# Loading later batches in four-head pieces, one piece per value sum, with q and k one more batch ahead

## The chip, the cores and the metric

The kernel runs on one core of a Trainium2 chip. The metric is device time in microseconds (us) for one launch, lower is better. Times of whole runs come from runs without a profiler; everything that is said of single instructions comes from one profiled execution.

## The reference

Eight batches of twelve heads, 448 positions and 64 channels per head go through a ReLU-squared attention without softmax; the result, seen as 3584 tokens of 768 channels, goes through a gated feed-forward block (GEGLU).

```python
scores = (1 / sqrt(64)) * q @ k.transpose(0, 1, 3, 2)
attn   = maximum(scores, 0) ** 2 / 448
x      = (attn @ v)                   # -> [3584, 768]
u      = gelu(x @ w_gate) * (x @ w_val)   # [3584, 1536], gelu with erf
out    = u @ w_out                    # [3584, 768]
```

Inputs and outputs are f32; the kernel computes in bf16 with f32 sums.

## The kernel before

**Tiling.** TensorE is used as four 64x64 quarters: two row halves (called PE0 and PE1 in the planner) that work at the same time, each with two column halves. A batch's feed-forward block is twelve chunks `fc` of 128 hidden channels. For each chunk `add_gate_value` (L411) adds a gate sum (g = 0), from which ScalarE makes the GELU `gel` (L429), and a value sum (g = 1), which VectorE multiplies into `uT` (L434). After the twelve chunks come output tiles of 128 tokens (`add_out`, L450), each in two halves that ScalarE copies into `osb` (L472, three buffers) and SyncE sends out as two DMAs (L477). By the loop at L516 batches 0 to 7 are followed by 2, 4, 3, 4, 3, 4, 3 and 5 output tiles.

**Attention.** A batch's attention is done during the feed-forward block of the batch before it: 21 score units (`add_scores`, L310; ReLU `rl` on ScalarE at L336, square on VectorE at L342) and six value products (`add_values`, L367; copy to `xT` on VectorE at L391).

**Loads.** All loads are GpSimd DMAs that cast f32 to bf16, in one queue in program order (`load`, L169; `load_qk`, L189; `load_v`, L204). Batches 0 and 1 come in pieces of two or four heads between the weights. Each later batch comes as four whole DMAs: q, k and two halves of v. q and k share a tile `qk16` of which there are two buffers, `v16` has two buffers as well. Batch b + 2 is put into the queue when the last value product of batch b is put into the work list (L544 to L549), q and k before v.

**Transposes.** Scores need q and k with channels on the partitions (`qkT`, two buffers). Batches 0 to 2 (`EARLY` = 3) are transposed by TensorE (`add_transposes`, L277, copies at L293). From batch 3 on (`add_dma_transposes`, L230) VectorE makes seven copies of `qk16` into `qkr` (L237, one buffer), and one DMA transpose from SyncE (L245) makes `qkT` of it. That transpose needs the buffer of `qkT` that the scores of two batches before have read.

**Order of the work.** The order on each engine is written out ahead of time by a small planner, `run_plan` (L23). Every piece of work is an `Op` with a cost, a list of others that it comes after, a lag and a priority. `PE0` and `POOL` are taken strictly in order; PE1, ACT, DVE and SP take, out of their next 48, the one that can start first, the smaller `prio` first among equals. Loads are given an arrival: bytes at 400 GB/s one after the other, and 2.0 us. A plan's dependence sets only the *order* of the instructions in the program; the semaphore waits on the chip come from the data alone (a tile's writer and readers, a free buffer, and eight semaphores that the loads take in turn, each only when its last load has landed). Each engine then runs its own list strictly in order: an instruction whose data is late holds back all that stand behind it on its engine.

Of the kernel before, what the change touches and what calls it, by code (L numbers as in the profile page):

```python
# [22 lines left out]
def run_plan(queues, pools, arrivals, together):  # L23

    free = {e: 0.0 for e in (*queues, *pools)}
    at = {e: 0 for e in queues}
    dma = last = floor = 0.0

    def ready(op):
        t = 0.0
        if op.after is not None:
            if op.after.start is None:
                return None
            t = op.after.start
        for d in op.deps:
            if d.end is None:
                return None
            t = max(t, d.end + d.lag)  # L40
        return t

    left = sum(map(len, queues.values())) + sum(map(len, pools.values()))
    while left:
        best = None
        for e, ops in queues.items():
            if at[e] < len(ops):
                r = ready(ops[at[e]])
                if r is not None:
                    t = max(r, free[e], floor if e in together else 0.0)  # L50
                    key = (t, 0, free[e])
                    if best is None or key < best[0]:
                        best = (key, e, ops[at[e]])
        for e, ops in pools.items():
            mine = None
            for op in ops[:48]:
                r = ready(op)
                if r is not None:
                    t = max(r, free[e], floor if e in together else 0.0)
                    key = (t, op.prio, free[e])  # L60
                    if mine is None or key < mine[0]:
                        mine = (key, e, op)
            if mine and (best is None or mine[0] < best[0]):
                best = mine
        assert best is not None, "the plan is stuck"
        (t, _, _), e, op = best
        op.start = t
        op.end = t + op.cost
        free[e] = op.end
        if e in together:  # L70
            floor = t
        if op in arrivals:
            dma = max(dma, op.end) + arrivals[op]
            op.lag = dma + 2.0 - op.end
        if e in at:
            at[e] += 1
        else:
            pools[e].remove(op)
        op.emit()
        last = max(last, op.end)  # L80
        left -= 1
    return last
# [3 lines left out]
def kernel(  # L86
# [16 lines left out]
    B, H, S, D = q.shape  # L103
# [3 lines left out]
    NPAIR = H // 2  # L107
# [12 lines left out]
    EARLY = 3  # L120
# [33 lines left out]
    def wait_lower(box):  # L154

        tc.add_manual_dep(nc.tensor.reg_mov(n_reg, 0).ins, box[1].ins.name, SYNC, reason="bank")

    ACT, DVE, POOL, SP = [], [], [], []
    arrivals = {}


# [4 lines left out]
    w12_op, wo_op, head_op = {}, {}, {}  # L166
    qk16, v16 = {}, {}

    def load(nbytes, emit, deps=(), cost=0.7):  # L169
        op = Op("POOL", cost, emit, deps)  # L170
        arrivals[op] = nbytes / 400e3
        POOL.append(op)
        return op
# [15 lines left out]
    def load_qk(b, i, h0, h1, deps=()):  # L189

        src = (q, k)[i]

        def tile_of():
            if b not in qk16:
                qk16[b] = qkv.tile([128, H * S // P * D], bf16, name="qk16", tag="qk16")
            return qk16[b][HALF[i], :]

        op = load(4 * (h1 - h0) * S * D, lambda: nc.gpsimd.dma_start(  # L198
            tile_of().rearrange("p (h x) -> p h x", h=H)[:, h0:h1, :],
            src[b, h0:h1].rearrange("h (p c) d -> p h (c d)", c=SC)), deps)  # L200
        for pr in range(h0 // 2, h1 // 2):
            head_op[b, pr, i] = op

    def load_v(b, h0, h1, deps=()):  # L204

        for i in range(2):
            def emit(i=i):
                if b not in v16:
                    v16[b] = qkv.tile([128, H, VC, D], bf16, name="v16", tag="v16")
                c0 = i * (SC - VC)  # L210
                nc.gpsimd.dma_start(  # L211
                    v16[b][HALF[i], h0:h1, :, :],
                    v[b, h0:h1].rearrange("h (p c) d -> p h c d", c=SC)[:, :, c0:c0 + VC, :])
            op = load(4 * (h1 - h0) * VC * P * D, emit, deps)
            for pr in range(h0 // 2, h1 // 2):
                head_op[b, pr, 2 + i] = op

    def load_heads(b, h0, h1, deps=((), ())):
        load_qk(b, 0, h0, h1, deps[0])
        load_qk(b, 1, h0, h1, deps[0])  # L220
        load_v(b, h0, h1, deps[1])

    qkT, tr_op, r_op = {}, {}, {}

    def qkT_tile(b):
        if b not in qkT:
            qkT[b] = tpool.tile([128, SC * NPAIR, 2 * P], bf16, name="qkT", tag="qkT")
        return qkT[b]

    def add_dma_transposes(b):  # L230

        box = {}

        def emit_copy(c):
            if not box:
                box[0] = lpool.tile([128, SC, H, D], bf16, name="qkr", tag="qkr")
            nc.vector.tensor_copy(  # L237
                box[0][:, c], qk16[b].rearrange("p (h c d) -> p c h d", c=SC, d=D)[:, c])

        copies = [Op("DVE", 0.4, lambda c=c: emit_copy(c),  # L240
                     [head_op[b, 0, 0], head_op[b, 0, 1], tr_op.get(b - 1)], lag=0.1, prio=3)
                  for c in range(SC)]
        DVE.extend(copies)
        r_op[b] = copies
        tr_op[b] = Op("SP", 7.0, lambda: nc.sync.dma_start_transpose(  # L245
            qkT_tile(b)[:, :, :], box[0].rearrange("p c h d -> p (c h d)")),
            [*copies, last_s.get(b - 2)], lag=5.0)
        SP.append(tr_op[b])


# [5 lines left out]
    def ring_dep():  # L256
        return [ring[-FB]] if len(ring) >= FB else []
# [15 lines left out]
    att, xT, last_s = {}, {}, {}  # L273
    t_op, relu_op, sq_op, o_op, x_op = {}, {}, {}, {}, {}
# [136 lines left out]
    def add_gate_value(at, b, fc, g):  # L411

        i, o = divmod(fc * 128, WCH)
        w = (wg, wv)[g][i]
        box = {}

        def emit(r, dc):
            if not box:
                box[0] = psF.tile([128, 512], f32, name="ff", tag="F")
            if r == 1 and dc == 0:  # L420
                wait_lower(box)
            for j in range(2):
                ins = mm(box[0][HALF[j], 0:S], w[HALF[r], dc, o + P * j:o + P * (j + 1)],
                         xT[b][HALF[r], dc, :], r, j, r == 0 and dc == 0, r == 1 and dc == KC - 1)
            box[1] = ins

        def emit_gelu():
            gel[b, fc] = gpool.tile([128, S], bf16, name="gel", tag="gel")
            nc.scalar.activation(gel[b, fc][:, :], box[0][:, 0:S], AF.Gelu)  # L429

        def emit_mult():
            if fc == 0:
                uT[b] = upool.tile([128, FC, S], bf16, name="uT", tag="uT")
            nc.vector.tensor_tensor(uT[b][:, fc, :], gel.pop((b, fc))[:, :],  # L434
                                    box[0][:, 0:S], op=ALU.mult)

        ops = [[Op(f"PE{r}", GS, lambda r=r, dc=dc: emit(r, dc),
                   [w12_op[i][g], x_op[b, dc], *(ring_dep() if r == 0 and dc == 0 else ())], lag=0.24)
                for dc in range(KC)] for r in range(2)]
        if g == 0:  # L440
            done = gel_op[b, fc] = Op("ACT", 0.55, emit_gelu, [ops[1][-1]], lag=0.06, prio=0)
            ACT.append(done)
        else:
            done = u_op[b, fc] = Op("DVE", 0.63, emit_mult, [gel_op[b, fc], ops[1][-1]],
                                    lag=0.1, prio=0)
            DVE.append(done)
        ring.append(done)
        then(at, GS, *ops, done)

# [91 lines left out]

    for at, _, fn, args in work:
        fn(at, *args)
        if fn is add_values and args[1] == NPAIR - 1 and args[0] + 2 < B:  # L544
            b = args[0]
            free = [t_op[b, NPAIR // 2 - 1, i] for i in range(2)] if b < EARLY else r_op[b]
            load_heads(b + 2, 0, H, (free, (o_op[b, NPAIR - 1],)))
            if b + 2 >= EARLY:
                add_dma_transposes(b + 2)  # L549


    def emit_filler():
# [6 lines left out]
    PE0 = [op for _, op in lower]  # L559
# [23 lines left out]
    PE1 = [op for _, op in upper]  # L583

    def emit_warm_up():
        t = psF.tile([128, 512], f32, name="ff", tag="F")
        for _ in range(10):
            for j in range(2):
# [1 line left out]
                                 start=True, stop=True, tile_position=(0, P * j))  # L590
    PE0.insert(0, warm_op)

    run_plan({"PE0": PE0, "POOL": POOL}, {"PE1": PE1, "ACT": ACT, "DVE": DVE, "SP": SP}, arrivals,
             ("PE0", "PE1"))


# [28 lines left out]
```

## Time and profile before

| | |
|---|---|
| time, median of 3 runs | 472.1 us (470.2 to 475.5) |
| time of the profiled execution | 468.75 us, of which the span of its instructions is 467.0 us |
| TensorE busy | 432.0 us, 93% of the span; granted clock 0.979 |
| VectorE, ScalarE busy | 206.2 us (44%), 225.5 us (48%) |
| GpSimd load queue | 36416 packets, 24.38 MB |
| SyncE queue (transposes, outputs) | 31520 packets, 17.90 MB |

How to read the rows that follow. A row of a timeline has start, duration, engine, line, operation, tiles written and read, and in brackets the idle time of the engine before it and what ended it. A row of waits has the engine and line that waited, what it waited for, and then us in total, how often, and the longest. A row of windows has for each engine its busy time and, behind x, its instructions, then the granted clock of TensorE, the share of the DMA engines' time and the GB/s moved. DMA rows have the count, the size in SBUF's type of one, and the median time from issue to landing. PE is TensorE's multiplications, PEld its weight loads, DVE VectorE, ACT ScalarE, POOL GpSimd, SP SyncE (SPq its queue).

### The profile page before, as it was taken

The page shows a single profiled execution, that of the slowest core. Times are in us where ns is not written, and L with a number is a line of the kernel's source. Part 1 is how long each engine was busy: PE and PEld are TensorE (multiplying, and loading weights), DVE is VectorE, ACT ScalarE, POOL GpSimd, SP SyncE. Part 2 cuts the span into 40 slices and gives each one's busy share as a digit, 9 for nine tenths or more (in the row PEclk, how much of TensorE's full clock was granted, in tenths as well). Part 3 has the DMA queues.
Part 4 walks back from the last instruction along what each step waited for, and adds up shares of the span by engine and source line. Part 5 has one row for each costly group of instructions (what it writes and reads, how often), then busy time and mean ns, then how long its engine had stood idle before and what let it go on. Part 6 is the DMA issues. An engine that isn't in the chain of part 4 may idle for free.

```text
span 467.0 us, 19995 instructions
## 1 busy us (share of the span) xinstructions
PE 432.0 (93%) x9360; PEld 370.6 (79%) x9360; DVE 206.2 (44%) x366; ACT 225.5 (48%) x322; POOL 48.9 (10%) x74
## 2 busy tenths in 40 slices
PE   6779999998997999996999959999999999999995
PEld 2547996976896678984999837899999978887895
DVE  1695655554542365443543334534553455312200
ACT  1686554444452555552555525555555555422221
POOL 8546300200002000020000100010000000000000
PEclk9998999999999899998999988999999999999998
DMA  7999999698029900695007950086002300030024
GB/s 101 192 198 198 205 207 193 88 158 136 1 48 167 232 4 3 119 207 85 3 3 132 221 94 1 3 163 129 3 3 54 88 3 4 14 93 3 3 70 102
DMA packets 68019, 43.56 MB, mean 93 GB/s; under 512 B 29024, under 2 KB 64352, under 8 KB 67936
## 3 DMA queue, kind: packets, MB, share of 16 engines
q0 software_dynamic: 36416, 24.38, 36.6%
q1 hardware_dynamic: 31520, 17.90, 18.0%
q8 instruction: 73, 1.20, 1.0%
q14 instruction: 10, 0.08, 0.1%
HBM read 48.76 MB, written 11.01 MB: 128 GB/s over the span
## 4 chain that ended last, share of the span: by engine, by line
PE 70%; DMA 22%; POOL 2%; issue 2%; DVE 2%; ACT 1%; SPq 0%; POOLq 0%; ACTq 0%; DVEq 0%
PE ff L151 64%; DMA qk<-in_k_dram 13%; PE sp L151 5%; DMA qk<-in_q_dram 3%; DMA wv<-in_moe_w_val_dram 2%; DMA out_dram<-osb 2%; DMA v<-in_v_dram 1%; POOL v L211 1%; POOL qk L198 1%; ACT rl L336 1%; DVE attnT L342 1%; DVE uT L434 0%; PE ff L287 0%; DVE qkT L293 0%; DVE qkr L237 0%
## 5 line engine op out<-in xcount | busy, mean ns | idle before, releaser
L151 PE MATMUL ff<-xT,wg 64*64 64x448 bf16 x2304 | 232.5, 356 | 13.9 <-DVE uT L434 9.6
L151 PE MATMUL ff<-xT,wv 64*64 64x448 bf16 x2304 | 232.0, 355 | 2.1 <-issue 2.1
L336 ACT ACTIVATE rl<-sp 128x896 bf16<-128x896 f32 x168 | 152.1, 920 | 126.7 <-PE sp L151 109.2
L151 PEld LDWEIGHTS <-wg 64*64 64x64 bf16 x2304 | 134.5, 109 | 34.1 <-issue 17.6
L151 PE MATMUL ff<-wo,uT 64*64 64x384 bf16 x2688 | 149.8, 323 | 0.3 <-DVE uT L434 0.2
L151 PEld LDWEIGHTS <-wv 64*64 64x64 bf16 x2304 | 134.8, 108 | 16.3 <-issue 1.2
L342 DVE TENSOR_TENSOR attnT<-rl 128x896 bf16<-128x896 bf16 x168 | 103.9, 623 | 89.7 <-ACT rl L336 88.9
L151 PEld LDWEIGHTS <-uT 64*64 64x64 bf16 x2688 | 124.9, 107 | 5.8 <-DVE uT L434 0.6
L151 PE MATMUL sp<-qkT 64*64 64x448 bf16 (+1 forms) x768 | 114.8, 348 | 7.8 <-ACT rl L336 4.7
L434 DVE TENSOR_TENSOR uT<-gel,ff 128x448 bf16<-128x448 bf16 x96 | 59.5, 620 | 78.5 <-PE ff L151 75.7
L151 PE MATMUL ff<-attnT,v 64*64 64x448 bf16 (+1 forms) x768 | 91.1, 338 | 0.0
L429 ACT ACTIVATE gel<-ff 128x448 bf16<-128x448 f32 x96 | 52.1, 543 | 63.5 <-PE ff L151 61.8
L151 PEld LDWEIGHTS <-qkT 64*64 64x64 bf16 x768 | 48.0, 111 | 19.4 <-issue 11.0
L151 PEld LDWEIGHTS <-v 64*64 64x64 bf16 x768 | 48.4, 110 | 4.0 <-issue 0.2
L472 ACT COPY osb<-ff 128x384 f32<-128x384 f32 x56 | 26.7, 477 | 46.3 <-PE ff L151 37.5
L391 DVE TENSOR_SCALAR xT<-ff 128x448 bf16<-128x448 f32 x48 | 29.9, 623 | 36.0 <-PE ff L151 31.3
L211 POOL DMA_DIRECT2D v<-in_v_dram x26 | 17.8, 703 | 245.5 <-PE sp L151 130.5
L287 PEld LDWEIGHTS <-qk 64*64 64x64 bf16 x504 | 14.3, 127 | 8.4 <-DMA qk<-in_k_dram 3.8
L287 PE MATMUL ff<-ident,qk 64*64 64x64 bf16 x504 | 15.2, 213 | 4.9 <-DMA qk<-in_k_dram 2.6
L237 DVE COPY qkr<-qk 128x768 bf16<-128x768 bf16 x35 | 11.5, 354 | 16.0 <-DMA qk<-in_k_dram 9.8
L293 DVE COPY qkT<-ff 128x896 bf16<-128x896 bf16 x18 | 10.9, 622 | 15.6 <-PE ff L287 11.7
L198 POOL DMA_DIRECT2D qk<-in_q_dram x13 | 9.3, 716 | 5.1 <-PE ff L287 2.8
(17 smaller groups left out, 32.5 us busy)
## 6 DMA issues: line engine op xcount, KB each, us to landing
out_dram<-osb SPq DMA_DIRECT2D x56, 192.0 KB, 4.0
v<-in_v_dram POOLq DMA_DIRECT2D x12, 384.0 KB, 9.8
qk<-in_q_dram POOLq DMA_DIRECT2D x6, 672.0 KB, 15.8
qk<-in_k_dram POOLq DMA_DIRECT2D x6, 672.0 KB, 19.0
wg<-in_moe_w_gate_dram POOLq DMA_DIRECT2D x6, 384.0 KB, 10.6
wv<-in_moe_w_val_dram POOLq DMA_DIRECT2D x6, 384.0 KB, 11.0
wo<-in_moe_w_out_dram POOLq DMA_DIRECT2D x4, 576.0 KB, 15.2
v<-in_v_dram POOLq DMA_DIRECT2D x10, 128.0 KB, 8.7
```

The costliest lines, as they stand in the source:

```text
L151: return nc.tensor.matmul(o, lhsT, rhs, start=start, stop=stop, tile_position=(P * row, P * col))
L198: op = load(4 * (h1 - h0) * S * D, lambda: nc.gpsimd.dma_start(tile_of().rearrange("p (h x) -> p h x", h=H)[:, h0:h1, :], src[b, h0:h1].re ...
L211: nc.gpsimd.dma_start(v16[b][HALF[i], h0:h1, :, :], v[b, h0:h1].rearrange("h (p c) d -> p h c d", c=SC)[:, :, c0:c0 + VC, :])
L237: nc.vector.tensor_copy(box[0][:, c], qk16[b].rearrange("p (h c d) -> p c h d", c=SC, d=D)[:, c])
L287: nc.tensor.transpose(t[HALF[j], pr, c * P:(c + 1) * P], src[HALF[i], 2 * (2 * m + pr) + j, c, :], ident[HALF[i], HALF[i]], tile_position= ...
L293: nc.vector.tensor_copy(dst[:, 2 * m:2 * m + 2, :, HALF[i]], box[i].rearrange("d r (c p) -> d r c p", c=SC))
L336: nc.scalar.activation(rl[:, :, :], box[0][:, :, 0:S], AF.Relu)
L342: nc.vector.tensor_tensor(a[:, :, :], box[1][:, :, :], box[1][:, :, :], op=ALU.mult)
L391: nc.vector.tensor_scalar_mul(xT[b][:, pr, :], box[0][:, 0:S], scalar1=out_scale)
L429: nc.scalar.activation(gel[b, fc][:, :], box[0][:, 0:S], AF.Gelu)
L434: nc.vector.tensor_tensor(uT[b][:, fc, :], gel.pop((b, fc))[:, :], box[0][:, 0:S], op=ALU.mult)
L472: nc.scalar.copy(ob[:, cols], box[0][:, 0:OGS])
```

## The change

The loads of later batches are hung on the value sums instead of on the end of a batch's attention. With each value sum of batch b (g = 1), chunk by chunk: chunks 0 to 5 put a piece of four heads of q (0 to 2), then of k (3 to 5), of batch b + 3 into the load queue; chunks 6 to 8 put a piece of four heads of v of batch b + 2 (two DMAs, one per half). Batch 2 is put in whole at the first chunk of batch 0. The DMA transpose of batch b + 2 and its copies are put in at chunk 0 of batch b. A new planner engine `IDLE`, which emits nothing, makes the plan put the copies at least 8 us behind the planned arrival of all of that batch's q and k, and the planned lag behind the transpose is 6 us instead of 5.

```diff
-    ACT, DVE, POOL, SP = [], [], [], []
+    ACT, DVE, POOL, SP, IDLE = [], [], [], [], []
...
-    def load_heads(b, h0, h1, deps=((), ())):
-        load_qk(b, 0, h0, h1, deps[0])
-        load_qk(b, 1, h0, h1, deps[0])
-        load_v(b, h0, h1, deps[1])
+    def load_heads(b, h0, h1):
+        load_qk(b, 0, h0, h1)
+        load_qk(b, 1, h0, h1)
+        load_v(b, h0, h1)
...
     def add_dma_transposes(b):
         box = {}
+        wait = Op("IDLE", 8.0, lambda: None, [head_op[b, pr, i] for pr in range(NPAIR) for i in range(2)])
+        IDLE.append(wait)
...
         copies = [Op("DVE", 0.4, lambda c=c: emit_copy(c),
-                     [head_op[b, 0, 0], head_op[b, 0, 1], tr_op.get(b - 1)], lag=0.1, prio=3)
+                     [wait, tr_op.get(b - 1)], lag=0.1, prio=3)
                   for c in range(SC)]
...
-            [*copies, last_s.get(b - 2)], lag=5.0)
+            [*copies, last_s.get(b - 2)], lag=6.0)
...
             done = u_op[b, fc] = Op("DVE", 0.63, emit_mult, [gel_op[b, fc], ops[1][-1]],
                                     lag=0.1, prio=0)
             DVE.append(done)
+            if EARLY <= b + 2 < B and fc == 0:
+                add_dma_transposes(b + 2)
+            if b == 0 and fc == 0:
+                load_heads(2, 0, H)
+            elif b + 2 < B and b and 6 <= fc < 9:
+                load_v(b + 2, 4 * (fc - 6), 4 * (fc - 5), [done])
+            if b + 3 < B and fc < 6:
+                h0 = 4 * (fc % 3)
+                load_qk(b + 3, fc // 3, h0, h0 + 4, [done])
...
     for at, _, fn, args in work:
         fn(at, *args)
-        if fn is add_values and args[1] == NPAIR - 1 and args[0] + 2 < B:
-            b = args[0]
-            free = [t_op[b, NPAIR // 2 - 1, i] for i in range(2)] if b < EARLY else r_op[b]
-            load_heads(b + 2, 0, H, (free, (o_op[b, NPAIR - 1],)))
-            if b + 2 >= EARLY:
-                add_dma_transposes(b + 2)
```

More of the change, by code (lines that the diff above doesn't have):

```diff
@@ L591 @@
     PE0.insert(0, warm_op)
-    run_plan({"PE0": PE0, "POOL": POOL}, {"PE1": PE1, "ACT": ACT, "DVE": DVE, "SP": SP}, arrivals,
+    run_plan({"PE0": PE0, "POOL": POOL}, {"PE1": PE1, "ACT": ACT, "DVE": DVE, "SP": SP, "IDLE": IDLE}, arrivals,
              ("PE0", "PE1"))
```

## The prediction

> **What bounds the kernel now.** I read the page first, for the engine with the least idle time, then windows laid batch by batch, then the waits, and only then the timelines around the gaps.
>
> ```profile
> span 467.0 us, 19995 instructions
> PE 432.0 (93%) x9360; PEld 370.6 (79%) x9360; DVE 206.2 (44%) x366; ACT 225.5 (48%) x322; POOL 48.9 (10%) x74
> ...
> 80.80:138.80 58.00, 54.68 (x1269) 47.17 (x1265) 29.24 (x57) 27.89 (x41) 2.99 (x4) 1.00 0.61 84
> 138.80:193.20 54.40, 50.17 (x1074) 40.99 (x1070) 25.05 (x46) 27.72 (x41) 3.00 (x4) 0.97 0.55 95
> 193.20:250.50 57.30, 52.76 (x1148) 48.62 (x1142) 25.54 (x46) 27.85 (x41) 3.00 (x4) 0.97 0.47 87
> 250.50:307.00 56.50, 51.34 (x1077) 42.82 (x1071) 24.99 (x46) 27.98 (x41) 3.00 (x4) 0.94 0.51 94
> 307.00:358.50 51.50, 51.47 (x1148) 49.06 (x1142) 23.76 (x39) 27.86 (x42) 1.50 (x2) 1.00 0.36 70
> 358.50:406.70 48.20, 48.09 (x1069) 41.45 (x1063) 23.39 (x39) 27.79 (x40) 0.00 (x0) 1.00 0.11 28
> ```
>
> The windows run from the first ReLU of a batch's scores to that of the next, for batches 2 to 7. The last two rows are the undisturbed kernel: TensorE busy all the time at full clock, 51.5 us with four output tiles, 48.2 with three. The third row has as many matmuls as the fifth and takes 5.8 us more; the fourth has the work of the sixth and takes 8.3 more. So TensorE is the bound, and the loss is its idle time plus the reduced clock behind it: idle 3.3, 4.2, 4.5 and 5.2 us in the first four rows, and 0.03 x 54.4 = 1.6, 0.03 x 57.3 = 1.7 and 0.06 x 56.5 = 3.4 us of clock in rows two to four. Rows one to four thus lose 3.3, 5.9, 6.3 and 8.5 us, 24 in all. Who ends those gaps?
>
> ```profile
> PE ff L151 <- DVE uT L434: 9.8, 3, 5.0
> PE ff L151 <- ACT osb L472: 4.1, 1, 4.1
> PE ff L151 <- issue: 2.1, 1, 2.1
> ...
> 216.29 0.63 DVE L237 COPY qkr<-qk 128x768 bf16<-128x768 bf16 x2 [5.69 <-DMA qk<-in_k_dram]
> 218.57 0.58 PE L151 MATMUL ff<-xT,wg 64*64 64x448 bf16 x2 [4.54 <-DVE uT L434]
> 275.41 0.63 DVE L237 COPY qkr<-qk 128x768 bf16<-128x768 bf16 x2 [6.16 <-issue]
> 277.42 0.59 PE L151 MATMUL ff<-xT,wg 64*64 64x448 bf16 x4 [5.05 <-DVE uT L434]
> ```
>
> Third and fourth windows: VectorE stands 5.7 and 6.2 us in front of the copy of q and k, whose k has not landed; `uT` behind it is late, its bank stays full, and TensorE stops for 4.54 and 5.05 us.
>
> ```profile
> 136.45 7.18 SPq L245 DMA_TRANSPOSE qkT<-qkr  x1
> 143.67 11.12 SPq L477 DMA_DIRECT2D out_dram<-osb  x8
> 144.01 1.50 POOL L211 DMA_DIRECT2D v<-in_v_dram  x2 [55.10 <-PE ff L151]
> 145.49 0.78 POOL L198 DMA_DIRECT2D qk<-in_q_dram  x1
> v<-in_v_dram POOLq DMA_DIRECT2D x1, 384.0 KB, 7.8
> DMA to landing us min/median/max: 3.1/5.4/7.6
> 151.98 0.48 ACT L472 COPY osb<-ff 128x384 f32<-128x384 f32 x1 [5.55 <-DMA out_dram<-osb]
> 152.51 0.38 PE L151 MATMUL ff<-xT,wg 64*64 64x448 bf16 x4 [4.11 <-ACT osb L472]
> ```
>
> Second window, another cause. The fourth output tile needs the first one's `osb` buffer. That tile's two output DMAs left SyncE only at 143.67 and 144.31, behind the transpose; the load of v began at 144.01 between them. The landing row is that of those two outputs: 3.1 us for the one ahead of the load, 7.6 for the one behind it. The latter lands at 151.9, and the first half of v, issued at 144.01 with 7.8 us to landing, at 151.8: the output lands with the whole load DMA ahead of it.
>
> **The change part by part.**
>
> *Does the gate pace the loads?* In the program's order only. On the chip a load waits for a free buffer, for its semaphore and for the load ahead in GpSimd's queue.
>
> ```profile
> 59.80 0.75 POOL L198 DMA_DIRECT2D qk<-in_k_dram  x1 [1.33 <-DMA wo<-in_moe_w_out_dram]
> 85.89 1.53 POOL L211 DMA_DIRECT2D v<-in_v_dram  x2 [25.34 <-PE sp L151]
> 87.41 0.75 POOL L198 DMA_DIRECT2D qk<-in_q_dram  x1
> 197.86 1.50 POOL L211 DMA_DIRECT2D v<-in_v_dram  x2 [50.85 <-PE sp L151]
> 200.07 0.79 POOL L198 DMA_DIRECT2D qk<-in_k_dram  x1
> qk<-in_k_dram POOLq DMA_DIRECT2D x1, 672.0 KB, 16.1
> ```
>
> Before, q and k of batch b + 3 stood behind v of batch b + 2, which waits until the values of batch b are done; so batch 6's k was issued at 200.07 and landed 16.1 us later, at 216.2, where VectorE already stood. After, the queue reads: q, k of 3; q, k of 4, v of 3; q, k of 5, v of 4; q, k of 6, v of 5; q, k of 7, v of 6. I follow the buffers: q and k of 4 start when batch 3's copies free a buffer (about 91), of 5 when batch 2's TensorE transposes end (about 117), of 6 right behind v of 4 (about 148), of 7 right behind v of 5 (about 200). For batches 5, 6 and 7 that is 28, 51 and 57 us sooner than the 145, 199 and 257 of before, and the plan puts their copies at least 8 us behind an arrival that the chip beats. **Both VectorE stalls go**: the 6.3 and 8.5 us of windows three and four, of which I leave 0.4 for the small gaps: **-14.4**. Batch 3's 3.58 us VectorE wait at 83.8 cost TensorE no gap, so I count nothing there.
>
> *The output that waits for a load.* Its place stays: v of batch 4 still starts when batch 2's values end, the transpose still holds SyncE for 7 us from the end of batch 2's scores, and q and k of batch 6 follow v as those of 5 did. What changes is the length of the DMA ahead: 128 KB instead of 384 KB. If the output's extra 4.5 us (7.6 - 3.1) are the load ahead of it, a third of it leaves 1.5: landing at 148.9 instead of 151.9, against a gap that began at 148.4. Bounds: 0, if the output waits for all pieces queued ahead, and the window's whole 5.9. I take 3.0 of the 4.1 us gap and the 1.6 of clock, since none of the clock's loss follows the shorter gap of 2.15 us in the first window: **-4.6**. The Trainium skill, "DMA: Bandwidth & Descriptors", section "Queues, rings and completion order", says that a DMA engine takes turns between queue rows by whole packets of at most 64 descriptors; by it 12 heads x 64 rows over 16 engines are 48 descriptors ahead of the output and four heads are 16, which gives the same third, and were a packet much shorter the pieces would change nothing here, the bound of 0.
>
> *The first window.* Here the transpose of batch 3 runs beside v of 3 and q, k of 4.
>
> ```profile
> 86.37 20.13 SPq L245 DMA_TRANSPOSE qkT<-qkr  x1
> qkT<-qkr SPq DMA_TRANSPOSE x1, 25.1
> 110.61 0.35 PE L151 MATMUL ff<-xT,wv 64*64 64x448 bf16 x1 [2.15 <-issue]
> 108.20 0.62 DVE L434 TENSOR_TENSOR uT<-gel,ff 128x448 bf16<-128x448 bf16 x1 [1.15 <-PE ff L151]
> DMA to landing us min/median/max: 9.8/10.0/25.1
> ```
>
> The 2.15 us gap waited for nothing that the trace names, in the middle of that crowd. The crowd stays and starts some 5 us later. Between 0 and the window's 3.3 on one side and as much again lost on the other (q, k of 5 add a transfer from 117) I take **-0.8**.
>
> *What is added.* Five batches of q, k and v come as 12 DMAs instead of 4, 40 issues more at 0.6 to 0.8 us of GpSimd.
>
> ```profile
> L211 POOL DMA_DIRECT2D v<-in_v_dram x26: 612/746/775, 2.9 to 312.4; - x26
> L293 DVE COPY qkT<-ff x18: 612/624/625, 9.1 to 116.8; 128x896 bf16<-128x896 bf16 x18
> DMA packets 7126, 3.96 MB, mean 198 GB/s; under 512 B 229, under 2 KB 7124, under 8 KB 7124
> ```
>
> That is at most 40 x 0.75 = 30 us on an engine that is busy for 10%; it is on no path as long as the loads are a batch early. VectorE is not slowed by GpSimd's issuing: its PSUM copies take 612 to 625 ns from 9 us on, while GpSimd issues without a pause, as at 116. Pieces do not slow the transfers: 20 to 40 us, all four-head pieces and weights, ran at 198 GB/s. The copies stay seven, on a VectorE that is 44% busy. More waits on PE and VectorE, one per piece: 0. Their cover is the spare batch; gone, the stalls of windows three and four are back.
>
> **Sum.** 14.4 + 4.6 + 0.8 = 19.8. Against the profiled execution 468.75 - 19.8 = 449.0; against the median of the runs, 3.35 us above it, 452.3. I forecast between the two, **451 us**.
>
> **Rivals.** (1) *The output still waits for loads*: SyncE's transpose and v of 4 keep their places, and all six pieces of v may stand ahead of it as the two halves did. For it: outputs behind v elsewhere land late as well. Only 14.4 to 15.2 go: 454 on the profiled execution, 457 on the median. (2) *Everything goes*, the first window too, as smaller pieces let outputs, transposes and TensorE's own instructions through: 24, so 445 to 448. Against it stands the crowd at 91 to 115. (3) *The loads do not run ahead*: if a buffer of q and k is handed out only when the batch that the planner names is copied, k lands under its copies again, and only the VectorE stalls shrink by little: 466 to 470. Against it: at 87.41 q of batch 4 went out while batch 2 was still being transposed (until 116), so a buffer goes to whoever finds one free. (4) *Slower: the copies of batch 4 wait for the transpose of batch 3*, which must have read `qkr`. Place: VectorE at chunk 10 of batch 1. The plan puts these copies 0.7 + 1.15 + 2.0 + 8.0 us (issue, a 0.46 MB piece at 400 GB/s, lag, idle wait) behind chunk 5's `uT`, which ended at 108.8, so at about 121; batch 3's transpose would start at 91 and, with 25.1 us, land at 116. Price: by window four a VectorE wait of 6.2 costs 8.5, 1.4 per us. It decides from a landing at about 135, 14 us of wait, a transpose of 44 us; at 50 us it costs 28, which ends at 477. For it: 25.1 us beside whole loads against 10.0 without, and now twelve DMAs take turns with it. By the Trainium skill's "DMA: Bandwidth & Descriptors", "Rules for kernel authors", transfers well under 1 MiB pay mostly a fixed cost and should be merged; with the 2 us that its section on the anatomy of a DMA gives, eight more DMAs per batch are 16 us (an estimate), which would stretch that crowd and speak for this rival. The 198 GB/s of the pieces at the start speak against the rule.
>
> **How the numbers follow.** Forecast 0.52 (446 to 456); rival 1 0.20 (453 to 459); rival 2 0.15 (443 to 448); rival 3 0.07; rival 4 0.06. Range: 443, the floor of rival 2, to 460, the top of rival 1; it leaves out rivals 3 and 4. About 1% (4.7 us) is what a measurement of this kernel can tell from no change: faster by more 0.87, within 0.07, slower 0.06.
>
> **What would show it.** Right: no VectorE wait of `qkr` for a DMA over 1 us; windows three and four at 51.5 and about 48.5 at full clock; q of batch 5 issued near 117; the fourth output tile of batch 1 waiting for its buffer under 2 us. Wrong: L237 still behind `in_k_dram` (rival 3) or behind the transpose (rival 4); a gap of 4 us at `osb` again (rival 1). What I can't see from here is whether the changed plan shuffles PE1 and VectorE into new small gaps; that would make the forecast wrong everywhere at once.

## The result, and the profile after

The changed kernel takes 455.98 us, median of four runs (450.72 to 456.21), where the kernel before took 471.47 in the same sessions. The ratio is 0.9631, with a 95% interval of 0.954 to 0.9722. The profiled execution took 456.05 us instead of 468.75, so 12.7 us less. The forecast was 451 us, range 443 to 460.

First the head of the page after (busy time by engine), then windows from the first ReLU of a batch's scores to that of the next, batches 2 to 7 as before, and under them the start of the program (up to batch 1's scores, and those) after and before.

```profile
span 454.2 us, 20046 instructions
PE 429.1 (94%) x9360; PEld 364.6 (80%) x9360; DVE 207.7 (46%) x366; ACT 226.0 (50%) x322; POOL 70.7 (16%) x114
```

```profile
82.50:140.90 58.40, 54.60 (x1268) 47.90 (x1264) 29.69 (x57) 27.82 (x40) 11.04 (x18) 1.00 0.77 104
140.90:190.30 49.40, 48.58 (x1078) 40.12 (x1071) 25.28 (x46) 27.81 (x41) 7.38 (x12) 1.00 0.61 106
190.30:241.10 50.80, 50.80 (x1145) 43.39 (x1140) 25.68 (x46) 27.86 (x41) 7.37 (x12) 1.00 0.54 97
241.10:293.70 52.60, 49.89 (x1077) 40.86 (x1071) 25.27 (x46) 27.95 (x40) 3.68 (x6) 0.97 0.39 75
293.70:345.70 52.00, 51.42 (x1150) 49.08 (x1146) 23.76 (x39) 27.95 (x42) 3.69 (x6) 1.00 0.35 69
345.70:394.00 48.30, 48.18 (x1071) 41.63 (x1066) 23.39 (x39) 27.91 (x40) 0.00 (x0) 1.00 0.11 28
...
0.00:33.00 33.00, 23.45 (x426) 14.80 (x427) 18.77 (x34) 19.05 (x22) 22.33 (x39) 0.74 1.18 160
33.00:82.50 49.50, 46.81 (x970) 38.80 (x971) 27.82 (x48) 26.38 (x35) 15.22 (x22) 0.90 1.29 199
```

```profile
0.00:33.80 33.80, 23.83 (x426) 14.92 (x427) 18.49 (x34) 18.82 (x23) 22.68 (x39) 1.00 1.18 162
33.80:80.80 47.00, 44.20 (x968) 37.44 (x969) 27.70 (x48) 26.23 (x34) 12.68 (x17) 0.96 1.31 203
```

The first column after the bounds is the length. Against before, batches 2 to 7 come out at +0.4, -5.0, -6.5, -3.9, +0.5 and +0.1 us. The start of the program is 1.7 us longer (82.5 instead of 80.8), at a lower granted clock. That makes -12.7 in all, by the windows. In the third window TensorE is busy for all of its 50.8 us; the fourth still has 2.7 us of idle time and a clock of 0.97.

The waits of the changed kernel (engine and line, releaser, us, times, longest):

```profile
ACT osb L484 <- DMA out_dram<-osb: 6.2, 2, 4.0
PE ff L151 <- ACT osb L484: 3.3, 2, 2.6
PE ff L290 <- issue: 3.0, 2, 2.5
PE ff L151 <- DVE uT L437: 0.2, 1, 0.2
```

No row of VectorE waiting with `qkr` for a DMA is left, and TensorE's 9.8 us behind `uT` are 0.2. Still there are a wait of 3.3 us in two places behind `osb`, and one of 2.5 us put down to nothing. The timelines of these two, after (start, duration, engine, line, operation, and in brackets the idle time before it):

```profile
245.94 5.58 SPq L489 DMA_DIRECT2D out_dram<-osb  x6
246.40 3.68 POOL L211 DMA_DIRECT2D v<-in_v_dram  x6 [42.22 <-PE ff L151]
252.84 0.48 ACT L484 COPY osb<-ff 128x384 f32<-128x384 f32 x1 [4.02 <-DMA out_dram<-osb]
253.37 0.59 PE L151 MATMUL ff<-xT,wg 64*64 64x448 bf16 x4 [2.58 <-ACT osb L484]
...
117.74 0.19 PE L290 MATMUL ff<-ident,qk 64*64 64x64 bf16 x1 [2.54 <-issue]
...
118.69 1.84 POOL L198 DMA_DIRECT2D qk<-in_q_dram  x3 [9.73 <-PE ff L151]
```

The wait for the output buffer has moved: it took 4.11 us in window two before, and takes 0.7 there and 2.58 in window four now, with SyncE's outputs and GpSimd's loads of v starting within half a microsecond of each other again. The last row is q of batch 5, issued at 118.69 (117 by the prediction's buffers).

### The profile page after: what moved, and what is told of

Its sections match the earlier page's. It is cut to its first block, busy times and chain, and to the rows that moved or that the text cites. A ratio compares the mean times of both kernels' runs of the same rounds, so it can differ in the third digit from the quotient of the medians.

```text
span 454.2 us, 20046 instructions
## 1 busy us (share of the span) xinstructions
PE 429.1 (94%) x9360; PEld 364.6 (80%) x9360; DVE 207.7 (46%) x366; ACT 226.0 (50%) x322; POOL 70.7 (16%) x114
## 4 chain that ended last, share of the span: by engine, by line
PE 87%; DMA 4%; ACT 3%; POOL 2%; issue 2%; DVE 2%; SPq 0%; ACTq 0%; POOLq 0%
PE ff L151 78%; PE sp L151 8%; DMA out_dram<-osb 2%; ACT rl L339 2%; DMA qk<-in_k_dram 2%; PE ff L290 1%; POOL qk L198 1%; POOL v L211 1%; DVE qkT L296 1%; DVE attnT L345 1%; ACT osb L484 0%; SPq L489 0%; DVE xT L394 0%; DVE uT L437 0%; POOL ident masks.py:199 0%
## 5 line engine op out<-in xcount | busy, mean ns | idle before, releaser
L151 PE MATMUL ff<-xT,wv 64*64 64x448 bf16 x2304 | 229.7, 351 | 0.4 <-issue 0.4
L211 POOL DMA_DIRECT2D v<-in_v_dram x46 | 28.8, 649 | 166.1 <-PE sp L151 87.8
L394 DVE TENSOR_SCALAR xT<-ff 128x448 bf16<-128x448 f32 x48 | 29.9, 624 | 39.2 <-PE ff L151 33.4
L198 POOL DMA_DIRECT2D qk<-in_q_dram x23 | 14.8, 653 | 41.0 <-DVE qkr L240 21.3
L198 POOL DMA_DIRECT2D qk<-in_k_dram x23 | 14.6, 644 | 14.4 <-DMA qk<-in_k_dram 4.3
```

What stands on the lines that cost most here:

```text
L151: return nc.tensor.matmul(o, lhsT, rhs, start=start, stop=stop, tile_position=(P * row, P * col))
L211: nc.gpsimd.dma_start(v16[b][HALF[i], h0:h1, :, :], v[b, h0:h1].rearrange("h (p c) d -> p h c d", c=SC)[:, :, c0:c0 + VC, :])
L394: nc.vector.tensor_scalar_mul(xT[b][:, pr, :], box[0][:, 0:S], scalar1=out_scale)
```

## The experiments

Three theories had to be told apart: the gain comes from q and k running a batch ahead; it comes from the planner's idle wait, which moves the seven copies back in VectorE's list; or it comes from the pieces. A second question was where the rest of the 24 us went.

### The idle wait alone

```diff
-    ACT, DVE, POOL, SP = [], [], [], []
+    ACT, DVE, POOL, SP, IDLE = [], [], [], [], []
...
+        wait = Op("IDLE", 8.0, lambda: None, [head_op[b, pr, i] for pr in range(NPAIR) for i in range(2)])
+        IDLE.append(wait)
...
-                     [head_op[b, 0, 0], head_op[b, 0, 1], tr_op.get(b - 1)], lag=0.1, prio=3)
+                     [wait, tr_op.get(b - 1)], lag=0.1, prio=3)
...
-            [*copies, last_s.get(b - 2)], lag=5.0)
+            [*copies, last_s.get(b - 2)], lag=6.0)
```

(on the kernel before: loads whole and at their old place)

> The kernel before with only the idle wait of 8 us ahead of the copies (and the lag of 6), loads whole and at their old place. The copies were reached 5.7 and 6.2 us too early, less than 8. If the place of the copies in VectorE's order is what counts, both stalls go without any load moved: the osb gap stays, 455 to 460. If the loads must be earlier: waits over 3 us at the copies stay and 465 to 471.

Measured: 449.8 us (447.79 to 451.63), ratio 0.9546 [0.9491, 0.9602]. Windows two to four, and VectorE where the copies of batch 6 now stand:

```profile
139.20:187.70 48.50, 48.38 (x1076) 41.61 (x1070) 25.26 (x46) 27.86 (x41) 2.98 (x4) 1.00 0.60 99
187.70:238.50 50.80, 50.80 (x1146) 43.30 (x1140) 25.68 (x46) 27.82 (x41) 2.99 (x4) 1.00 0.55 96
238.50:286.90 48.40, 48.28 (x1079) 41.83 (x1073) 25.27 (x46) 27.93 (x41) 3.00 (x4) 1.00 0.58 112
...
212.51 0.62 DVE L437 TENSOR_TENSOR uT<-gel,ff 128x448 bf16<-128x448 bf16 x1 [1.13 <-PE ff L151]
213.05 0.62 DVE L345 TENSOR_TENSOR attnT<-rl 128x896 bf16<-128x896 bf16 x1
213.59 0.89 DVE L240 COPY qkr<-qk 128x768 bf16<-128x768 bf16 x3
```

The loads keep their old place, and the copies stand behind a `uT` and a square which no longer wait for them. So the place of seven copies in an in-order list was the whole of the two VectorE stalls; the running ahead isn't needed for them. Window two, without a VectorE stall to lose, is 5.9 us shorter as well. SyncE's queue at its end shows why, with the landings of the first two outputs:

```profile
135.27 1.12 SPq L480 DMA_DIRECT2D out_dram<-osb  x2
136.92 7.12 SPq L248 DMA_TRANSPOSE qkT<-qkr  x1
...
DMA to landing us min/median/max: 2.6/2.7/2.7
```

With the copies later the transpose is later in the plan, and the first tile's outputs go ahead of it instead of behind. That is a by-product of the plan, and it is part of the 0.9546; with it the time came out 5 us under the 455 to 460 of the theory, which had kept the `osb` gap. This one part of the change, at 449.8 us, is no slower than the whole change with 455.98: the ratios are 0.9546 and 0.9631, with intervals that overlap.

### The change without the idle wait

```diff
-        IDLE.append(wait)
...
-                     [wait, tr_op.get(b - 1)], lag=0.1, prio=3)
+                     [*(head_op[b, pr, i] for pr in range(NPAIR) for i in range(2)), tr_op.get(b - 1)], lag=0.1, prio=3)
```

> The change without the idle wait: copies planned at the planned arrival of all of q and k. If the batch ahead alone is enough: no wait of the copies of batches 5 to 7 (batch 3's 3 to 4 us wait is back and costs TensorE nothing), 450 to 457. If the idle wait is what removes the stalls: waits of 4 us and more for batches 4 to 7 and 462 or more.

Measured: 455.85 us (453.02 to 459.39), ratio 0.968 [0.9608, 0.9751]. Its waits:

```profile
PE ff L151 <- issue: 5.8, 1, 5.8
PE ff L151 <- ACT osb L483: 1.2, 1, 1.2
PE ff L151 <- DVE uT L436: 0.2, 1, 0.2
```

The VectorE stalls are gone here too: with the loads a batch ahead, the old place is late enough. Each of the two measures takes the stalls away by itself; the change has both. What this one loses is the unnamed gap of the first window, 5.8 us of it, with 6 us at half clock behind it.

### Less idle wait

```diff
-        wait = Op("IDLE", 8.0, lambda: None, [head_op[b, pr, i] for pr in range(NPAIR) for i in range(2)])
+        wait = Op("IDLE", 4.0, lambda: None, [head_op[b, pr, i] for pr in range(NPAIR) for i in range(2)])
```

(on the kernel with the idle wait alone)

> The kernel before with the idle wait alone, of 4 us instead of 8. Theory (what cost time was the place of seven copies in VectorE's order, some 5.7 and 6.2 us too early, of which about 1.15 us are covered by TensorE's full banks): VectorE waits of qkr for k of 1.5 to 2.5 us stay in windows three and four, TensorE gaps behind uT of 0.5 to 1.5 us each; 451 to 454 us where the 8 us gave 449.8. Rival (the wait is all or nothing, or the gain of 8 us came from the outputs that its plan put ahead of the transpose): VectorE waits of 5 us, or none, and a gap of 1.5 us or more at osb; 454 to 460 us.

Measured: 456.12 us (453.56 to 458.96), ratio 0.9729 [0.9681, 0.9777].

```profile
DVE qkr L240 <- DMA qk<-in_k_dram: 7.5, 3, 3.1
PE ff L151 <- DVE uT L437: 2.5, 3, 1.2
PE ff L151 <- issue: 2.2, 2, 1.3
PE ff L151 <- ACT osb L475: 1.3, 1, 1.3
```

Half the distance leaves VectorE waits of up to 3.1 us and TensorE gaps of up to 1.2, in windows three and four, near the 1.5 to 2.5 and the 0.5 to 1.5 of the theory. The profiled execution, 453.56 us, lies in the theory's range; the median lies 2 us above it, in that of the rival. A wait for `osb` was there as well, which the rival had and the theory had not. So the time doesn't tell the two apart; the waits of half the length do, as far as the VectorE stalls go, and SyncE's queue shows the rest:

```profile
136.69 7.03 SPq L248 DMA_TRANSPOSE qkT<-qkr  x1
143.77 2.79 SPq L480 DMA_DIRECT2D out_dram<-osb  x4
```

The shorter wait has the transpose ahead of the outputs again, as in the kernel before.

### Pieces alone

```diff
-        load_qk(b, 0, h0, h1, deps[0])
-        load_qk(b, 1, h0, h1, deps[0])
-        load_v(b, h0, h1, deps[1])
+        step = 4 if b > 2 else h1 - h0
+        for i in range(2):
+            for h in range(h0, h1, step):
+                load_qk(b, i, h, h + step, deps[0])
+        for h in range(h0, h1, step):
+            load_v(b, h, h + step, deps[1])
```

(on the kernel before)

> The kernel before with batches 3 to 7 loaded in four-head pieces at their old place in the queue, no batch ahead, no idle wait. If running ahead matters: the two VectorE stalls of 5.7 and 6.2 us stay, and only the osb gap of 4.1 us shrinks to under 1.5, so 463 to 468. If the pieces matter: 451 to 458.

Measured: 481.86 us (480.67 to 484.58), ratio 1.0219 [1.0164, 1.0275]. A miss for both theories, with its cause in the plan: the copies are planned behind `head_op[b, 0, ...]`, which is now the first piece alone, so they stood still earlier. VectorE waited 29.9 us in four places:

```profile
DVE qkr L240 <- DMA qk<-in_k_dram: 29.9, 4, 8.6
```

With the one line

```diff
-                     [head_op[b, 0, 0], head_op[b, 0, 1], tr_op.get(b - 1)], lag=0.1, prio=3)
+                     [*(head_op[b, pr, i] for pr in range(NPAIR) for i in range(2)), tr_op.get(b - 1)], lag=0.1, prio=3)
```

added, so that the plan waits for all pieces:

> As the run with pieces alone, but the copies are planned behind the arrival of all pieces of q and k instead of the first one of each. If pieces alone were slow because the plan put the copies behind the first piece: VectorE waits back to 5 to 6 us at two places and 466 to 474, as the kernel before. If pieces in themselves slow the loads: over 476.

Measured: 470.96 us over ten runs (466.12 to 473.54), ratio 0.9984 [0.993, 1.0039].

```profile
DVE qkr L240 <- DMA qk<-in_k_dram: 19.2, 4, 5.9
```

Pieces at the old place do not change the time. The stalls are there as before (19.2 us in four places, where the kernel before had 16.0 in four), and so is the time that they cost. The run before this one is a dose of its own, the other way: the same loads, the copies earlier still, 11 us more.

### The change with whole loads

```diff
-            elif b + 2 < B and b and 6 <= fc < 9:
-                load_v(b + 2, 4 * (fc - 6), 4 * (fc - 5), [done])
-            if b + 3 < B and fc < 6:
-                h0 = 4 * (fc % 3)
-                load_qk(b + 3, fc // 3, h0, h0 + 4, [done])
+            elif b + 2 < B and b and fc == 6:
+                load_v(b + 2, 0, H, [done])
+            if b + 3 < B and fc in (0, 3):
+                load_qk(b + 3, fc // 3, 0, H, [done])
```

> The change with whole loads (twelve heads: q at chunk 0, k at chunk 3, v at chunk 6) in place of four-head pieces; q and k still a batch ahead. If running ahead removes the VectorE stalls and the pieces only shorten the output that waits for a load: no wait of the qkr copies over 1 us, and a gap of about 4 us at osb with half clock behind it in one or both of the stages of batches 3 and 5, so 458 to 464. If the pieces are what removes the VectorE stalls: waits of 5 to 6 us at L240 again and 466 to 471. If pieces are of no use anywhere: 451 to 456, as the changed kernel.

Measured: 456.28 us (450.79 to 458.34), ratio 0.9646 [0.9561, 0.9731]: the change's 0.9631. That is 0.3 us above the range of the theory in which pieces are of no use, and 1.7 under that of the theory in which they shorten the output. Its waits, and the landings of the first tile's two outputs beside the load of v (384 KB and 8.1 us to landing, issued at 148.28; the outputs at 147.77 and 148.41):

```profile
PE ff L151 <- ACT osb L483: 3.7, 2, 2.1
PE ff L290 <- issue: 3.3, 2, 2.8
...
DMA to landing us min/median/max: 4.1/4.7/5.3
...
v<-in_v_dram POOLq DMA_DIRECT2D x1, 384.0 KB, 8.1
```

The same two kinds of gap, 3.7 and 2.8 us, where the pieces had 3.3 and 2.5 (the profiled execution took 458.34 us, so its order of events is used here, not its total). The output issued 0.13 us behind the whole load landed at 153.7, 2.7 us *before* it. So it doesn't wait for the load ahead of it; it is slowed while both run. Even in this execution window two is 50.3 us long (143.0 to 193.3), against 54.4 before and 49.4 in the change: most of what the change gained there needs no pieces.

### Loads held back on the chip

```diff
+    def gated(ins, gate):
+        if gate is not None:
+            tc.add_manual_dep(ins.ins, u_ins[gate].ins.name, SYNC, reason="gate")
...
-                load_v(b + 2, 4 * (fc - 6), 4 * (fc - 5), [done])
+                load_v(b + 2, 4 * (fc - 6), 4 * (fc - 5), [done], (b, fc))
...
-                load_qk(b + 3, fc // 3, h0, h0 + 4, [done])
+                load_qk(b + 3, fc // 3, h0, h0 + 4, [done], (b, fc))
```

(on the change; `u_ins` holds the product of each chunk, and every load issue waits for that of its chunk)

> The change with its gates made real: each later load waits on the chip for the uT product of its chunk, instead of the plan's order alone. If the crowd of loads, transpose and TensorE's instruction blocks near 95 to 118 us makes the unnamed gap of 2.5 us, and if loads that start with the values' end make the output wait: no osb gap over 0.3 us, v of batch 4 issued near chunk 6 of batch 2 (about 170) and not at 146, unnamed gap under 1, in all 448 to 452. If the loads have nothing to do with either gap: 455 to 458. If pacing makes data late: VectorE or value waits and over 460.

Measured: 447.48 us (447.08 to 447.99), ratio 0.9499 [0.9431, 0.9568]. No wait of TensorE for `osb` is left, v of batch 4 goes out from 168 us on instead of 146, and the unnamed gap is 1.2 us, where under 1 was expected. The same with whole loads, gated at chunks 0, 3 and 6:

> Loads whole (q at chunk 0, k at chunk 3, v at chunk 6), q and k one batch further ahead, idle wait, and each load held back on the chip until the product of its chunk. Theory (pacing on the chip is what helps, and the pieces do nothing): within 1% of the same kernel with pieces, 446 to 451 us; the transpose of batch 3 under 16 us of issue. Rival (pieces matter once they are paced, since a whole load stands ahead of outputs and of TensorE's instructions for longer): 452 to 456 us, an output behind v landing after 5 us or more, a gap at osb or of unnamed cause over 2 us.

Measured: 446.3 us (445.5 to 447.64), ratio 0.9503 [0.9475, 0.953]: the lowest time of all, and the pieces make no difference when paced either. Windows of this one for batches 2 to 6, the landings of its DMA transposes and, last, of all its outputs (min/median/max):

```profile
81.90:137.90 56.00, 54.61 (x1269) 47.37 (x1265) 29.68 (x57) 27.84 (x41) 2.97 (x4) 1.00 0.58 85
137.90:186.30 48.40, 48.28 (x1074) 41.57 (x1070) 25.17 (x46) 27.78 (x40) 2.97 (x4) 1.00 0.67 107
186.30:237.20 50.90, 50.90 (x1148) 43.43 (x1142) 25.68 (x46) 27.88 (x42) 2.97 (x4) 1.00 0.58 96
237.20:285.50 48.30, 48.18 (x1075) 41.85 (x1070) 25.18 (x46) 27.87 (x40) 2.98 (x4) 1.00 0.62 112
285.50:336.40 50.90, 50.90 (x1148) 49.22 (x1142) 23.80 (x39) 27.86 (x41) 1.49 (x2) 1.00 0.37 71
...
DMA to landing us min/median/max: 9.8/10.0/17.6
...
DMA to landing us min/median/max: 2.6/2.8/4.6
```

Four of the five windows are now at their floor (48.3 with three output tiles, 50.9 with four), and the first is 2.4 us shorter than in the change. Before, outputs landed after up to 9.9 us and the transpose of batch 3 after 25.1. In the change:

```profile
DMA to landing us min/median/max: 2.6/4.0/8.5
...
DMA to landing us min/median/max: 8.7/9.8/27.3
```

The pairs that differ in nothing but the hold on the chip are the change and the first of these (0.9631 to 0.9499) and the two with whole loads (0.9646 to 0.9503): 6 to 7 us by the ratios, 8.5 to 10 by the medians. The intervals of the second pair are apart, those of the first overlap a little. The spread of the runs goes with it: 0.9 and 2.1 us instead of 5.5 and, without its one run of 458.34, 5.7. Against the idle wait alone (0.9546) the two are lower by half a per cent, with intervals that overlap, so a gain over that kernel is not shown.

### Four output buffers

```diff
-    opool = ctx.enter_context(tc.tile_pool(name="opool", bufs=3))
+    opool = ctx.enter_context(tc.tile_pool(name="opool", bufs=4))
```

> The change with four osb buffers instead of three. The fourth output tile of batches 1 and 3 then waits for no output. If the osb wait costs what the trace shows (0.7, and 2.6 with 1.7 of clock behind it): 5 us less than the change's 456 for runs like the profiled one, 449 to 453. If the outputs delay something else (SyncE's queue, the transposes): 455 to 458.

Measured: 450.02 us (449.61 to 454.35), ratio 0.9574 [0.9474, 0.9673], and no TensorE wait of `osb` left. The median says 6 us; the interval overlaps that of the change, so the size is not settled. The same on top of the held loads:

> The change with each load held back on the chip until the product of its chunk, and four output buffers instead of three. Theory (with paced loads no output waits, so the fourth buffer has nothing left to take away): 446 to 449 us, the same as with three. Rival (outputs that wait still set the start of some work): 443 to 446 us.

Measured: 449.03 us (448.2 to 450.85), ratio 0.9563 [0.9532, 0.9594]. No gain, as the theory said. The median is 1.5 us above that with three. The profiled executions differ by 3.4 us, and 2.9 of them lie before the scores of batch 2 (84.5 us against 81.6), where no output has been made yet.

### A longer warm-up

```diff
-        for _ in range(10):
+        for _ in range(18):
```

(on the change)

> The change with 36 warm-up matmuls instead of 20, which should bridge the 3.3 us in which TensorE waits for the second q piece, so that the clock isn't halved from 7 to 24 us. If the early half clock cost the time by which the profiled run missed the forecast: 451 to 453 and a granted clock of 0.98 or more in every run. If the start is bound by the loads whatever the clock: 455 to 457 at the higher clock.

Measured: 456.11 us (451.14 to 457.66), ratio 0.9664 [0.9546, 0.9782]. TensorE still ran at half clock from 11.1 us for 13.7 us and from 35.0 for 6.8. So the test doesn't decide what the early half clock costs. A bound comes from other pairs: the held loads with pieces began batch 2's scores at 81.6 us, at a clock of 0.998 for the run, and those with whole loads at 81.9, with half clock at the start and 0.969. And the four runs of the held loads with pieces have clocks from 0.998 to 0.968 and times within 0.9 us.

## Why the prediction was right, and where it was not

**The VectorE stalls (-14.4).** Right as to which stalls cost what and that they go, and q of 5, 6 and 7 were issued at 118.69, 150.05 and 198.54 where the working said 117, 148 and 200. Window three gave 6.5 of its 6.3. Window four gave 3.9 of 8.5, because 2.6 us of waiting for `osb` and, behind it, 3.4 us at half clock appeared in it. That is not the stall coming back but the next wait in line, and the prediction had not asked what was late next in that window: v of batch 6 and the outputs had been 0.20 us apart there before, the output ahead (255.58 against 255.78, landed after 3.2 us). In the change it is 0.13 us behind (246.53 against 246.40) and lands after 6.2. Of the signs that the prediction set itself, the VectorE waits, window three and q of batch 5 came true, and the fourth output tile of batch 1 just missed (2.1 us for its buffer, where under 2 was asked). Window four did not come true, and the 4.0 us of ScalarE in front of `osb` there are the sign of rival 1.

**"Their cover is the spare batch; gone, the stalls are back."** Wrong. With the spare batch gone and the idle wait kept, they stay away. The working gave the whole to the earlier landing and passed over the later place of the copies, though it named the 8 us.

**The output that waits for a load (-4.6).** The size fitted window two (-5.0), the reason failed, so the fit was luck. The step had the output land "with the whole load DMA ahead of it", so that a third of the load would leave a third of the extra time. With whole loads and all else alike, window two still gave 4.1 of the 5.0 us, the output landed 2.7 us before the load, and the gaps at `osb` were 3.7 us against 3.3.

In the ten profiled executions without held loads, an output that started up to 0.3 us behind the first load of v, with no other load under way, landed after 4.1 to 6.2 us where that load was a piece (ten cases), and after 4.0 to 7.6 where it was whole (nine). The 7.6, the worst of them, is the one that the step was worked out from. An output up to 0.3 us ahead of the load landed after 3.2 to 3.7 us in 18 of 23 cases and after 4.0 to 5.0 in the others. So what counts most is which of the two starts first, by tenths of a microsecond, and no dependence of the plan holds one behind the other. The prediction put the rule from the Trainium skill, "DMA: Bandwidth & Descriptors", section "Queues, rings and completion order", on the side of a third, with packets of up to 64 descriptors. The same passage gives 9 to 17 as typical, and with packets as short as those the pieces change nothing; the landings above show no difference that can be told from their scatter.

**The first window (-0.8).** It gave +0.4. The crowd did not stay as it was: batch 3's transpose, in among twelve pieces, took 27.3 us instead of 25.1, and the unnamed gap 2.54 instead of 2.15. With the loads held back it is 57.0 us (pieces) and 56.0 (whole) instead of 58.4, with the idle wait alone 56.5; that part of rival 2 was to be had, and not by piece size.

**What is added (0).** Right for the pieces, which cost nothing in either pair. The start is 1.7 us longer, at a granted clock of 0.74 and 0.90 instead of 1.00 and 0.96. No step had that. The kernel with the idle wait alone, whose loads are those of before, began batch 2's scores at 82.7 us too, so the earlier loads need not be behind it; what is stays open.

**The rivals.** Rival 1 (the output still waits) had the right symptom; it foresaw it in window two, for the six pieces, and it came in window four, by the order of issue. Its 454 to 457 holds the 455.98 that was measured; the forecast's 446 to 456 just does. Rival 2 (everything goes) is what the held loads reached, 446.3 to 447.5. Rival 3 did not happen. Rival 4 neither, and its margin was small: batch 3's transpose landed at 122.27, and the copies of batch 4 began at 123.74 with no wait.

In one line, on the profiled execution: -19.8 expected, -12.7 measured; of the 7.1 missing, 4.0 are the output wait of window four less what window three gave over, 1.2 the first window, and 2.2 the start and what comes behind window four, against 0.4 more in window two (each rounded).

## What to carry to other kernels

When an engine that works strictly in order stands in front of late data, first ask whether the instruction can stand later in its list: here that alone gave 0.9546, against 0.968 for loading a batch earlier without it and 0.9631 for both. Transfers that are issued as soon as a buffer is free crowd those that somebody waits for; a load a batch ahead has time to spare, and holding it back on the chip until its place took 6 to 10 us off the change, while cutting it into pieces took off nothing. Held back, the loads a batch ahead come out level with the later copies alone, within the intervals (0.9499 and 0.9503 against 0.9546): here the first question was nearly the whole answer. A plan that gives only the order doesn't pace anything: check in the trace of the queue when a transfer starts, and what else starts within half a microsecond of it.

## What the runs showed of the hardware that was not expected

**TensorE stops with its data there.** The gap of 2.54 us before 117.74 was put down to "issue". In the DMA view of 114 to 115 us, after, a third queue shows one packet of instructions among the loads and the transpose (queue, kind: packets, MB, share):

```profile
q0 software_dynamic: 241, 0.12, 84.5%
q1 hardware_dynamic: 253, 0.06, 47.4%
q8 instruction: 1, 0.02, 8.4%
```

It began at 114.8 and took 1.3 us; TensorE went on 1.6 us after its end. The same holds for every gap of over 0.3 us behind the first 40 us that the traces put down to "issue", 36 in the thirteen profiled executions: each ended 1.2 to 1.7 us after the end of such a packet, of which each execution has 73, about one in 6 us. Among them are the gaps of the kernel before (2.15 us), with whole loads (2.81) and without the idle wait (5.82); with the loads held back the longest are 0.5, 1.2 and 1.7 us. The Trainium skill, "Runtime: NRT & Kernel Launch", section "Instruction fetch mechanics", has instructions fetched by DMA in 16 KiB blocks, at a cost that is mostly hidden; the 16 KB packets agree, the hiding did not hold in this crowd. That the late block is the cause is argued from these times; no experiment took it alone.

**Half clock after a gap of under 3 us.** Behind the wait of 2.58 us that ended at 253.37:

```profile
253.00:256.40 3.40, 3.03 (x36) 1.83 (x39) 0.63 (x1) 2.16 (x4) 0.00 (x0) 0.50 1.18 279
```

3.4 us at a granted clock of 0.50, so 1.7 us lost. The gap of 2.54 us in the first window was followed by none (clock 1.00 in that row). Over the thirteen profiled executions, behind the first 45 us, all eleven gaps of TensorE of 3.6 us or more came with a stretch at half clock, five of the ten between 1.6 and 2.9 us did, and none of the shorter ones. So the prediction's step from one gap of 2.15 us, that a short gap costs no clock, held for that gap and is no rule. The Trainium skill, "TensorE: Matmul & The Clock Gate", section "What's actually happening", puts the drop behind at least one idle window of about 3.4 us; the stretch has that length, but gaps of 1.6 to 2.8 us were enough in five cases here.
